# Centroid norms from matmuls, and the second pair's inputs in the set-up, in a kernel of clustered attention and two MLPs

## The chip, the core and the metric

The kernel runs on one core of a Trainium2 chip. Times are device microseconds of one execution. The kernel is compared with its changed version by the median of several executions. A profiled execution gives the trace; its times run from the start of the span, which is the first to the last instruction.

The engines are called PE (TensorE; PEld its weight loads), DVE (VectorE), ACT (ScalarE), POOL (GpSimd) and SP (SyncE, which here only issues DMAs).

## The reference

Inputs are fp32: `q`, `k`, `v` of 2 batches x 8 heads x 768 positions x 64, and 16 centroids of 64 numbers for every head. Each query and each key goes to the centroid that it is most like, and a query attends only to keys of its own cluster. Two MLPs follow, on 1536 tokens of 512 features.

```python
q_assign = np.argmax(np.einsum('bhsd,hcd->bhsc', q_n, c_n), axis=-1)   # q_n, c_n: divided by norm + 1e-6
k_assign = np.argmax(np.einsum('bhsd,hcd->bhsc', k_n, c_n), axis=-1)
mask = q_assign[:, :, :, None] == k_assign[:, :, None, :]
scores = np.where(mask, scale * np.matmul(q, k.transpose(0, 1, 3, 2)), -1e9)
attn = exp(scores - max) ; attn = attn / (sum(attn) + 1e-9)
x = (attn @ v).reshape(1536, 512)
x = silu(x @ w_in) @ w_out                    # 512 -> 2048 -> 512
out = (sigmoid(x @ w_gate) * (x @ w_val)) @ w_out2   # 512 -> 1536 -> 512
```

The choice needs the norm of each centroid only: the norm of a query changes none of its 16 products' order.

## The kernel before

**Pairs and tiles.** Two heads of one batch are a pair; there are `NPAIR` = 8. A pair's queries lie as 128 x 768 (64 features of head `j` = 0 on partitions 0 to 63, of `j` = 1 on 64 to 127). A pair has 12 tiles: 2 heads x 6 blocks of 128 queries. `scores(p, j, i)` (line 463) makes one: four matmuls into a PSUM tile `s` of two banks (high and low parts of queries and keys in `qa`, `ka`; masks and the rest in `qm`, `km`), the maximum `nm` on DVE (L476), the exponential `e` on ACT (L481). `transposes` turns `e` (PE; copied out by ACT or DVE into `ph`), `values` multiplies by `v` for three tiles at a time.

**PSUM.** Pool `ps_s` has two buffers of two banks, `ps_t` three of one bank, `ps_v` one of one bank. A tile takes a free buffer of its pool and gives it back after the last use of it in the program; the next tile waits for that. So with two buffers of `ps_s`, tile n + 2 of the scores waits for the exponential of tile n.

**Choosing clusters.** `product_of_clusters` multiplies queries and keys by the centroids `cc` (four fp32 matmuls on four column strips, L157), `scaled` applies the factor `unit` (the inverse norm of the centroid, L277), `similarities` turns the result back by three transposes (L168), and DVE picks the largest of 16 and makes one-hot rows `oh` (`first_choice` for pair 0, one head at a time; the steps of `prep(p)` at L422 for the others). `choice_rows` turns these on PE, `query_rows` and `key_rows` write them into `qm` and `km`, where they act as the mask inside the scores' matmuls.

**Set-up** (lines 186 to 621). Between `first.__enter__()` and `first.__exit__()` the instructions of PE, DVE, ACT and SP stand in their queues as written. The order on SP: `cr` (centroids, 128 KB), the first pair's queries `qq` and keys `kk`; ACT's queue loads `cc`, zero outside two blocks. Norms: `csq` = `cr` squared, summed on DVE into `n2`, the square root on ACT (L268), then six small steps on DVE to `unit` (L274). Queries and keys are split into high and low parts (`qh`, `ql`, `kh`), which SP copies into `qa`, `ka`, `qm`. `warm(n)` issues `n` matmuls of 512 columns on zeros into a PSUM tile `pw` that nothing reads (L210); `WARM` = (10, 1, 8, 5) are its four counts: at the start, behind the first product, behind `similarities`, and behind the scores of the first two tiles, which end the set-up.

**Steady part.** `one_tile` runs for the 12 tiles of each pair; only PE's order is written out there. The other engines' order is found by a scheduler that simulates, with some instructions tied behind others by `issue_after`. For pair 0, tiles 0 to 5, all that DVE gets beside the maxima stands behind tile 1's maximum. `prep(p + 1)` gets the next pair ready in steps between the tiles of pair p: POOL splits its queries and keys (L395 ff.), SP copies them, PE multiplies its clusters (`clusters`), and DVE makes the masks. The second pair's inputs are loaded by `load(1)` at the end of the set-up.

The MLPs follow on PE in a written order, with weights that are converted from the fp64 form by ACT, POOL and DVE ahead of use.

Of the kernel before, what the change touches and what calls it, by code (L numbers as in the profile page):

```python
# [27 lines left out]
WARM = (10, 1, 8, 5)  # L28
# [3 lines left out]
def clustered_attention_then_two_mlps(ctx, tc, qT, kT, v, cen, cenT, w1i, w1o, w2g, w2v, w2o, out):  # L32
    nc = tc.nc
    B, HP, _, S = qT.shape
    D = cen.shape[2]
# [73 lines left out]
    with ExitStack() as att:  # L109
# [80 lines left out]
        act_dma = nc.scalar.dma_start  # L190
        cr = cp.tile([P, HP, D], F32, tag="cr", name="cr")
        dma(cr, cen)
        cc = cp.tile([P, HP, 2, C], F32, tag="cc", name="cc")
        nc.vector.memset(cc, 0.0)
        for j, r in enumerate((L, U)):
            act_dma(cc[r, :, j], cenT[j])
# [5 lines left out]

# [3 lines left out]
        pw = ps_v.tile([P, 512], F32, tag="v", name="pw")  # L206
# [5 lines left out]
        warm(WARM[0])  # L212
# [13 lines left out]

        sq = sm.tile([P, 1], F32, tag="sq", name="sq", bufs=1)
        nc.vector.memset(sq, 1.0)
        nc.scalar.activation(sq, sq, AF.Sqrt)
# [32 lines left out]
        csq = cp.tile([P, HP, D], F32, tag="csq", name="csq")  # L262
        nc.vector.tensor_tensor(csq, cr, cr, op=ALU.mult)
        n2, r0, r1, r2, r3, r4 = (norm(f"r{n}") for n in range(6))
        unit = cp.tile([P, HP], F32, tag="unit", name="unit")
        nc.vector.tensor_reduce(n2, csq, axis=AX.X, op=ALU.add)
# [20 lines left out]
        nc.vector.tensor_tensor(km[L, 0], kk[L], kh[L], op=ALU.subtract)  # L287

        for j, (r, o) in enumerate(((L, U), (U, L))):
# [3 lines left out]
            dma(qa[o, j].bitcast(F32), ql[r].bitcast(F32))  # L293
# [12 lines left out]
        similarities(ps, sums)  # L306
        warm(WARM[2])

        chosen = []

        def first_choice(j, seen):
# [4 lines left out]
            for n in range(2):  # L316
                nc.vector.tensor_tensor(
# [4 lines left out]
                )  # L322

# [27 lines left out]
        for _ in first_choice(0, ps[:, 0:HS]):  # L351
            pass
        cast(nc.scalar, sums, ps[:, 0:HS])
# [16 lines left out]
        query_rows(0, pts[1], 0, half, half)  # L370

        on_pool = {}

        first_products = {}

        def clusters(p):
            sim = wk.tile([P, NT, 2, 2, C], F32, tag="sim", name=f"sim{p}", bufs=1)
            pm = ps_t.tile([P, 512], F32, tag="t", name=f"pm{p}")
            product_of_clusters(pm, p, *raws[p][:2])
            scaled(p, sim.rearrange("p t n j c -> p (t n j c)"), pm[:, 0:HS])  # L380
            first_products[p] = sim

        def prep(p):
# [11 lines left out]
            nc.gpsimd.tensor_scalar(qq, qq, scale, 1.0, op0=ALU.mult, op1=ALU.mult)  # L395
# [3 lines left out]
            cast(nc.gpsimd, kh, kk)  # L399
# [12 lines left out]
            sim = first_products.pop(p)  # L412
            sums = sim.rearrange("p t n j c -> p (t n j c)")
# [200 lines left out]
        if NPAIR > 1:  # L614
            load(1)
            load_values(1)
        tiles = [(p, j, i) for p in range(NPAIR) for j in range(2) for i in range(NT)]
        for t in tiles[:2]:
            scores(*t)
# [585 lines left out]
```

## Time and profile before

| | |
|---|---|
| median of 3 runs | 772.26 us (771.88 to 773.91) |
| profiled execution, span | 770.1 us; its own whole time is not listed, the median is 2.16 us above the span |
| PE busy | 760.9 us (99%) |
| DVE busy | 620.1 us (81%) |
| ACT busy | 403.4 us (52%) |
| POOL busy | 393.8 us (51%) |
| chain that ended last | PE 92%, DVE 3%, ACT 2%, DMA 1%, issue 1% |
| instructions | 11463 |

Busy time of PE counts from the start of each matmul to an end that is modelled, so that consecutive matmuls overlap: the distance of two starts is the better price of one. An idle time in brackets names the engine that ended it. The chain of waits is followed back from the last instruction to what released each step.

### The profile page before, as it was taken

What the parts mean: (1) busy time and instruction counts of PE and PEld (TensorE: products, weight loads), DVE (VectorE), ACT (ScalarE), POOL (GpSimd) and SP (SyncE); (2) the same over time, 40 slices, a digit from 0 to 9 for tenths busy, and PEclk for the clock granted to TensorE, in tenths of its full rate; (3) what the DMA queues carried; (4) which work ended last, traced back from release to release, by engine and by line L of the source; (5) the groups of instructions that cost most, each with busy time, mean ns of one, the idle gap of its engine ahead of it and who ended that gap; (6) DMA issues with size and microseconds to landing.
All of it is one profiled execution on the core that took longest, in us unless ns stands there. A gap on an engine that the chain in (4) does not pass through costs nothing.

```text
span 770.1 us, 11463 instructions
## 1 busy us (share of the span) xinstructions
PE 760.9 (99%) x4314; PEld 652.6 (85%) x4314; DVE 620.1 (81%) x787; ACT 403.4 (52%) x691; POOL 393.8 (51%) x345
## 2 busy tenths in 40 slices
PE   8999999999999999999999999999999999999998
PEld 4766777677768998998989989998998989899896
DVE  6887887788787968798978669996596997979645
ACT  6777776777886672543524516546442425344120
POOL 5235134643655773476646525644573937748320
PEclk9999999999999999999999999999999999999999
DMA  7677457447122122132222111221111221121004
GB/s 207 167 210 194 113 147 195 120 125 201 32 76 83 55 82 85 53 110 82 89 77 83 55 54 60 93 69 56 40 70 55 83 83 55 55 83 55 1 0 164
DMA packets 25488, 71.61 MB, mean 93 GB/s; under 512 B 4484, under 2 KB 4952, under 8 KB 25432
## 3 DMA queue, kind: packets, MB, share of 16 engines
q1 hardware_dynamic: 24888, 70.84, 31.1%
q8 instruction: 34, 0.56, 0.3%
q14 instruction: 22, 0.18, 0.1%
q10 hardware_dynamic: 544, 0.03, 0.0%
HBM read 48.01 MB, written 3.19 MB: 66 GB/s over the span
## 4 chain that ended last, share of the span: by engine, by line
PE 92%; DVE 3%; ACT 2%; DMA 1%; issue 1%; POOL 0%; SPq 0%; ACTq 0%
PE z L1021 13%; PE s L468 8%; PE v L518 7%; PE t L505 5%; PE y L962 4%; PE h_0w L846 4%; PE h_0x L846 4%; PE g_0w L846 3%; PE g_0x L846 3%; PE v_0w L846 3%; PE v_0x L846 3%; PE r L912 2%; PE q L912 2%; PE y_00None L962 2%; PE y_20None L962 2%; PE y_11None L962 2%
## 5 line engine op out<-in xcount | busy, mean ns | idle before, releaser
L481 ACT ACTIVATE e<-s,nm 128x768 f32<-128x768 f32 x96 | 86.5, 901 | 33.8 <-DVE nm L476 32.7
L476 DVE TENSOR_REDUCE nm<-s 128x1 f32<-128x768 f32 x96 | 91.4, 953 | 10.3 <-PE s L468 8.6
L1021 PE MATMUL z<-wu,ghb 128*128 128x512 f32 (+1 forms) x292 | 89.5, 388 | 0.0
L518 PE MATMUL v<-ph,vv 128*64 128x384 f32 x384 | 69.0, 494 | 0.2 <-DVE xf L530 0.2
L1021 PEld LDWEIGHTS z<-wu,ghb 128*128 128x128 f32 x292 | 54.2, 188 | 11.7 <-ACT ghb L64 0.6
L468 PE MATMUL s<-ka,qa 128*128 128x384 f32 x192 | 57.5, 380 | 1.7 <-ACT e L481 1.3
L505 PE MATMUL t<-ident,e 128*128 128x128 f32 x384 | 58.4, 275 | 0.1
L1021 PE MATMUL z<-wu,glb 128*128 128x512 f32 (+1 forms) x146 | 56.9, 390 | 0.0
L505 PEld LDWEIGHTS t<-ident,e 128*128 128x128 f32 x384 | 44.9, 140 | 11.3 <-issue 9.0
L518 PEld LDWEIGHTS v<-ph,vv 128*64 128x64 f32 x384 | 24.7, 136 | 32.8 <-issue 29.0
L468 PE MATMUL s<-k,q 128*128 128x384 f32 x192 | 49.7, 339 | 0.0
L942 DVE TENSOR_TENSOR acc<-z,acc 128x1024 f32<-128x1024 f32 (+2 forms) x32 | 36.6, 1152 | 13.8 <-PE z L1021 13.2
L64 ACT ACTIVATE ph<-t 128x512 f32<-128x512 f32 x68 | 40.6, 598 | 12.4 <-PE t L505 11.9
L67 DVE COPY ph<-u 128x512 f32<-128x512 f32 x48 | 32.8, 682 | 16.3 <-PE u L495 16.3
L549 POOL TENSOR_TENSOR acc<-xf,rb 128x768 f32<-128x768 f32 x7 | 12.9, 1837 | 58.5 <-DMA rb<-d_rb 40.0
L741 POOL TENSOR_TENSOR wo<-co,wo 128x512 fp32r<-128x512 f32 x16 | 23.5, 1471 | 33.6 <-ACT wo L64 33.6
L468 PEld LDWEIGHTS s<-k,q 128*128 128x128 f32 x192 | 34.5, 188 | 0.5 <-ACT k L338 0.3
L468 PEld LDWEIGHTS s<-ka,qa 128*128 128x128 f32 x192 | 28.9, 190 | 6.9 <-ACT e L481 6.0
L1021 PEld LDWEIGHTS z<-wu,glb 128*128 128x128 f32 x146 | 27.4, 188 | 6.9 <-DVE glb L902 1.4
L962 PE MATMUL y<-gha,wo 128*128 128x384 f32 x128 | 32.8, 334 | 0.0
L530 DVE TENSOR_TENSOR xf<-v,other 64x384 f32<-64x384 f32 x32 | 17.7, 553 | 14.8 <-ACT other L527 14.3
L395 POOL TENSOR_SCALAR qq<-qq 128x768 f32<-128x768 f32 x7 | 5.9, 838 | 38.2 <-PE pm L157 22.3
(629 smaller groups left out, 2160.3 us busy)
## 6 DMA issues: line engine op xcount, KB each, us to landing
ri<-in_w1i SPq DMA_DIRECT2D x16, 512.0 KB, 3.2
ro<-in_w1o SPq DMA_DIRECT2D x16, 512.0 KB, 3.2
ka<-kh SPq DMA_DIRECT2D x32, 192.0 KB, 3.4
rg<-in_w2g SPq DMA_DIRECT2D x12, 512.0 KB, 3.2
rv<-in_w2v SPq DMA_DIRECT2D x12, 512.0 KB, 3.2
ru<-in_w2o SPq DMA_DIRECT2D x12, 512.0 KB, 3.2
qq<-in_qT SPq DMA_DIRECT2D x8, 384.0 KB, 3.7
kk<-in_kT SPq DMA_DIRECT2D x8, 384.0 KB, 4.3
```

Source lines behind the costliest of these rows:

```text
L64: return nc.scalar.activation(o, i, AF.Copy)
L67: return nc.vector.tensor_copy(o, i)
L468: nc.tensor.matmul(s[:, g, 0:HS], lhsT=a[:, j, i * P : (i + 1) * P], rhs=c[:, j, g * HS : (g + 1) * HS], start=n == 0, stop=n == 1,)
L476: maxima.append(nc.vector.tensor_reduce(nm, s[:, :, 0:HS], axis=AX.XY, op=ALU.max, negate=True))
L481: x = nc.scalar.activation(e, s[:, :, 0:HS], AF.Exp, bias=nm, scale=1.0, accum_out=tots[p][:, n : n + 1])
L505: nc.tensor.transpose(t[:, kt, :], e[:, kt * P : (kt + 1) * P], ident)
L518: m = nc.tensor.matmul(o[(L, U)[kt % 2]], lhsT=vv[:, j, kt, :], rhs=ring[:, kt, g * G : (g + 1) * G], start=n < 2, stop=n >= NT - 2,)
L846: nc.tensor.matmul(o[:, b, 0:HS], lhsT=w[a][s][:, k, :], rhs=right[b, q][t][:, k, :], start=start and k == 0 and n == 0, stop=k == KQ - 1 ...
L912: nc.tensor.matmul(o[:, h, 0:HS], lhsT=w[f"a{m + 1}{r + 1}"][s][:, k, :], rhs=right[b, f"{r + 1}{h + 1}"][t][:, k, :], start=r == 0 and k ...
L942: added.append(nc.vector.tensor_tensor(z, o, z, op=ALU.add))
L962: nc.tensor.matmul(o[:, d, 0:width], lhsT=s[:, d, k, :], rhs=t[:, c], start=k == 0 and m == 0, stop=k == 1 and m == 2,)
L1021: nc.tensor.matmul(o[:, a, c], lhsT=s[:, q * P : (q + 1) * P], rhs=r[:, c], start=k == 0 and m == 0, stop=k == 1 and m == 2, skip_group_ch ...
```

## The change

- `cen` is no longer an input. `cs` loads the transposed centroids (`cenT`, 64 features x 16 centroids per pair of heads, both heads on 128 partitions); DVE copies them into the two blocks of `cc`, squares `cc`, and PE sums the squares over the partitions by multiplying with a column `one`: for each of 4 pairs of heads and each of 4 strips of 32 partitions one matmul, into the PSUM tile `n2`.
- The ten warm-ups at the start are split, five before and five behind these matmuls. `WARM` becomes (10, 1, 4, 3).
- The second pair's queries and keys are loaded right behind the first pair's, into `acc`, which is free until the attention writes there. Their product with the centroids (`ahead`) stands on PE behind the similarities of pair 0, its scaling on ACT behind the query rows, its transposes (`seen`) on PE behind the scores of tile 1, and the cast of these on DVE. `prep(1)` then leaves these steps out; `load(1)` goes.
- `pw` is a tile of `ps_s`; `ahead` is one of `ps_v`.
- The low part of the first head's keys is computed on POOL (it was DVE, L287); the first copy of `ql` is cut in two halves.
- POOL's first steps for pair 1 are tied behind the last choice mask of pair 0.

```diff
 SIGN = -0x80000000
-WARM = (10, 1, 8, 5)
+WARM = (10, 1, 4, 3)
 @with_exitstack
-def clustered_attention_then_two_mlps(ctx, tc, qT, kT, v, cen, cenT, w1i, w1o, w2g, w2v, w2o, out):
+def clustered_attention_then_two_mlps(ctx, tc, qT, kT, v, cenT, w1i, w1o, w2g, w2v, w2o, out):
     nc = tc.nc
     B, HP, _, S = qT.shape
-    D = cen.shape[2]
+    D = cenT.shape[1]
     H = 2 * HP
...
-        act_dma = nc.scalar.dma_start
-        cr = cp.tile([P, HP, D], F32, tag="cr", name="cr")
-        dma(cr, cen)
+        cs = cp.tile([P, HP, C], F32, tag="cs", name="cs")
+        dma(cs, cenT.rearrange("j d h c -> (j d) h c"))
         cc = cp.tile([P, HP, 2, C], F32, tag="cc", name="cc")
         nc.vector.memset(cc, 0.0)
-        for j, r in enumerate((L, U)):
-            act_dma(cc[r, :, j], cenT[j])
         qq = raw.tile([P, S], F32, tag="qq", name="qq0")
         dma(kk, kT[0, 0])
-
+        raws[1] = tuple(acc[:, HP - 1, n].rearrange("p b s -> p (b s)") for n in range(2))
+        for t, a in zip(raws[1], (qT, kT)):
+            dma(t, a[divmod(1, HP)])
         nc.vector.memset(wt, 0.0)
-        pw = ps_v.tile([P, 512], F32, tag="v", name="pw")
+        pw = ps_s.tile([P, 512], F32, tag="s", name="pw")
-        warm(WARM[0])
+        warm(WARM[0] // 2)
         ident = cp.tile([P, P], F32, tag="ident", name="ident")
...
+        one = sm.tile([P, 1], F32, tag="one", name="one", bufs=1)
+        nc.vector.memset(one, 1.0)
         sq = sm.tile([P, 1], F32, tag="sq", name="sq", bufs=1)
-        nc.vector.memset(sq, 1.0)
-        nc.scalar.activation(sq, sq, AF.Sqrt)
+        nc.scalar.activation(sq, one, AF.Sqrt)
...
-        csq = cp.tile([P, HP, D], F32, tag="csq", name="csq")
-        nc.vector.tensor_tensor(csq, cr, cr, op=ALU.mult)
-        n2, r0, r1, r2, r3, r4 = (norm(f"r{n}") for n in range(6))
+        for j, r in enumerate((L, U)):
+            nc.vector.tensor_copy(cc[r, :, j], cs[r])
+        csq = cp.tile([P, HP, 2, C], F32, tag="csq", name="csq")
+        nc.vector.tensor_tensor(csq, cc, cc, op=ALU.mult)
+        r0, r1, r2, r3, r4 = (norm(f"r{n}") for n in range(5))
         unit = cp.tile([P, HP], F32, tag="unit", name="unit")
-        nc.vector.tensor_reduce(n2, csq, axis=AX.X, op=ALU.add)
+        n2 = ps_t.tile([P, HP], F32, tag="t", name="n2")
+        for h in range(HP):
+            for n in range(4):
+                nc.tensor.matmul(
+                    n2[32 * n : 32 * n + 32, h : h + 1],
+                    lhsT=csq[:, h].rearrange("p j c -> p (j c)"),
+                    rhs=one,
+                    start=True,
+                    stop=True,
+                )
+        warm(WARM[0] - WARM[0] // 2)
         nc.scalar.activation(identb, ident, AF.Copy)
...
         cast(nc.scalar, kh, kk)
-        nc.vector.tensor_tensor(km[L, 0], kk[L], kh[L], op=ALU.subtract)
+        nc.gpsimd.tensor_tensor(km[L, 0], kk[L], kh[L], op=ALU.subtract)
             dma(ka[U, j].bitcast(F32), kh[r].bitcast(F32))
-            dma(qa[o, j].bitcast(F32), ql[r].bitcast(F32))
+            for c in (slice(0, HS), slice(HS, S)) if j == 0 else (slice(0, S),):
+                dma(qa[o, j, c].bitcast(F32), ql[r, c].bitcast(F32))
             if j:
...
         similarities(ps, sums)
+        ahead = ps_v.tile([P, 512], F32, tag="v", name="pm1")
+        product_of_clusters(ahead, 1, *raws[1])
         warm(WARM[2])
...
             for n in range(2):
-                nc.vector.tensor_tensor(
+                last = nc.vector.tensor_tensor(
                     oh[0][:, :, j, n, 0:C],
                 )
+            chosen.append(last)
...
             pass
+        chosen.pop()
         cast(nc.scalar, sums, ps[:, 0:HS])
...
         query_rows(0, pts[1], 0, half, half)
+        sim1 = acc[:, 0, 0, B - 1, :]
+        scaled(1, sim1, ahead[:, 0:HS])
+        first_products = {1: sim1}
-        first_products = {}
-
         def clusters(p):
-            sim = wk.tile([P, NT, 2, 2, C], F32, tag="sim", name=f"sim{p}", bufs=1)
+            sim = wk.tile([P, HS], F32, tag="sim", name=f"sim{p}", bufs=1)
             pm = ps_t.tile([P, 512], F32, tag="t", name=f"pm{p}")
             product_of_clusters(pm, p, *raws[p][:2])
-            scaled(p, sim.rearrange("p t n j c -> p (t n j c)"), pm[:, 0:HS])
+            scaled(p, sim, pm[:, 0:HS])
             first_products[p] = sim
+
+        def seen(p, sums, eng):
+
+            ps = ps_t.tile([P, 512], F32, tag="t", name=f"ps{p}")
+            similarities(ps, sums)
+            cast(eng, sums, ps[:, 0:HS])
...
-            nc.gpsimd.tensor_scalar(qq, qq, scale, 1.0, op0=ALU.mult, op1=ALU.mult)
+            with tc.issue_after(chosen[-1].ins) if p == 1 else nullcontext():
+                nc.gpsimd.tensor_scalar(qq, qq, scale, 1.0, op0=ALU.mult, op1=ALU.mult)
             cast(nc.gpsimd, qh, qq)
             yield
-            cast(nc.gpsimd, kh, kk)
+            with tc.issue_after(chosen[-1].ins) if p == 1 else nullcontext():
+                cast(nc.gpsimd, kh, kk)
             on_pool["split", p] = nc.gpsimd.tensor_tensor(kl, kk, kh, op=ALU.subtract)
...
                 clusters(p)
-            sim = first_products.pop(p)
-            sums = sim.rearrange("p t n j c -> p (t n j c)")
-            yield
-            ps = ps_t.tile([P, 512], F32, tag="t", name=f"ps{p}")
-            similarities(ps, sums)
-            cast(nc.scalar, sums, ps[:, 0:HS])
+            sums = first_products.pop(p)
+            yield
+            if p > 1:
+                seen(p, sums, nc.scalar)
             yield
...
             W = 4 * NT
-            sg = sim.rearrange("p t n j c -> p (t n j) c")
+            sg = sums.rearrange("p (w c) -> p w c", c=C)
             queued(one, nc.vector.tensor_reduce, mk[:, 0, :], sg, axis=AX.X, op=ALU.max)
...
-        if NPAIR > 1:
-            load(1)
-            load_values(1)
+        load_values(1)
         tiles = [(p, j, i) for p in range(NPAIR) for j in range(2) for i in range(NT)]
             scores(*t)
+        seen(1, sim1, nc.vector)
         warm(WARM[3])
...
         "v": v.reshape(B, H // 2, 2, S // P, P, D).transpose(0, 1, 4, 2, 3, 5),
-        "cen": np.broadcast_to(cen.transpose(1, 2, 0, 3), (2, 2, *cen.shape[1:3], H // 2, D)).reshape(P, H // 2, D),
         "cenT": cen.transpose(1, 3, 0, 2),
```

## Rows read from the trace of the kernel before

**Rows 1.** Busy time of every engine in stretches of 50 us: stretch, us busy and instructions, clock.

```profile
0.00:50.00 50.00, 45.97 (x285) 29.45 (x286) 38.49 (x95) 36.10 (x70) 21.79 (x28) 1.00 0.74 187
50.00:100.00 50.00, 50.00 (x342) 35.73 (x341) 39.46 (x57) 36.09 (x73) 16.58 (x13) 1.00 0.67 173
```

**Rows 2.** Timeline of DVE, 12 to 31.5 us: start, duration, operation, idle before it.

```profile
12.70 1.82 DVE L476 TENSOR_REDUCE nm<-s 128x1 f32<-128x768 f32 x2 [1.09 <-PE s L468]
...
15.75 0.96 DVE L476 TENSOR_REDUCE nm<-s 128x1 f32<-128x768 f32 x1 [0.29 <-PE s L468]
...
24.98 0.96 DVE L476 TENSOR_REDUCE nm<-s 128x1 f32<-128x768 f32 x1 [0.59 <-PE s L468]
...
29.02 0.94 DVE L476 TENSOR_REDUCE nm<-s 128x1 f32<-128x768 f32 x1
```

**Rows 3.** Chain that ended last, 0 to 45 us: start, duration, what ran.

```profile
13.70 1.00 ACT e L481 x2
...
14.74 0.97 PE s L468 x4
...
23.26 0.33 PE ps L168 x3
...
31.04 0.96 PE s L468 x4
```

**Rows 4.** Timeline of the first 8 us: centroid loads, first keys.

```profile
2.82 0.43 DVE L263 TENSOR_TENSOR csq<-cr 128x256 f32<-128x256 f32 x1 [0.69 <-DMA cr<-in_cen]
...
6.00 0.84 ACT L64 ACTIVATE kh<-kk 128x768 fp32r<-128x768 f32 x1 [0.30 <-DMA kk<-in_kT]
```

**Rows 5.** Timeline, TensorE: warm-ups, first product, the first tile's last wait.

```profile
1.32 4.45 PE L210 MATMUL pw<-wt 128*128 128x512 bf16 x10 [1.32 <-DVE sq L228]
...
6.28 0.48 PE L157 MATMUL pm<-qq,cc 128*32 128x384 f32 x1 [0.52 <-DMA cc<-in_cenT]
...
8.30 1.89 PE L210 MATMUL pw<-wt 128*128 128x512 bf16 x8
...
12.22 0.19 PEld L468 LDWEIGHTS s<-k,q 128*128 128x128 f32 x1 [0.26 <-ACT k L338]
```

**Rows 6.** Timeline, TensorE at 234 us: 12 small fp32 matmuls (two records each).

```profile
234.50 1.75 PE L597 MATMUL rb<-ident,rs 128*64 128x128 f32 x24
```

**Rows 7.** Timeline: weight loads of the first product.

```profile
6.25 0.14 PEld L157 LDWEIGHTS pm<-qq,cc 128*32 128x32 f32 x2 [1.39 <-DMA cc<-in_cenT]
...
6.33 0.11 PEld L157 LDWEIGHTS pm<-kk,cc 128*32 128x32 f32 x1
```

**Rows 8.** Timeline: the norms' square root, the factors, the first scaled products.

```profile
3.94 0.19 ACT L268 ACTIVATE r<-r 128x4 f32<-128x4 f32 x1
...
5.18 0.18 DVE L274 RECIPROCAL unit<-r 128x4 f32<-128x4 f32 x1
...
7.22 0.58 ACT L277 ACTIVATE sim<-pm,unit 128x384 f32<-128x384 f32 x1 [0.38 <-PE pm L157]
```

**Rows 9.** Windows of half a microsecond: last figures are DMA share and GB/s.

```profile
4.00:4.50 0.50, 0.50 (x3) 0.16 (x2) 0.30 (x2) 0.13 (x2) 0.00 (x0) 1.00 1.03 389
```

**Rows 10.** Timeline: choice rows, query rows, a copy on DVE, pair 1's product.

```profile
10.64 0.55 PE L325 MATMUL pt<-identb,oh 128*64 128x128 bf16 x7 [0.45 <-DVE oh L317]
...
12.19 0.74 ACT L328 ACTIVATE q<-pt 16x256 fp32r<-16x256 bf16 x2
...
18.82 0.68 DVE L67 COPY ph<-t 128x512 f32<-128x512 f32 x1
...
20.64 0.51 PE L157 MATMUL pm<-qq,cc 128*32 128x384 f32 x1
```

**Rows 11.** Timeline, 21 to 40 us: what follows the product, pair 1's last copy and scores.

```profile
21.42 0.44 PE L495 MATMUL u<-ident,e 128*128 128x128 f32 x2
...
29.52 0.61 SPq L408 DMA_DIRECT2D k<-kl  x1
...
36.36 0.60 PE L468 MATMUL s<-ka,qa 128*128 128x384 f32 x2
```

## The prediction

> **What bounds the kernel now.** I read the windows of 50 us first, then the chain of waits, then the timeline of the stretch where these two part. From 50 us on TensorE (PE) has no idle time, before that it has 4 us of it [rows 1]. So after the set-up and the first tiles nothing can be won or lost but by PE work, and a delay that is still there when PE becomes continuous stays to the end. The question is when that is. The chain of waits changes there: at 13.70 an exponential and at 14.74 the third tile's scores that wait for its buffer; the last such step is the scores at 31.04, behind the exponential of tile 8, and from there the chain runs on PE [rows 3]. I count the 12 tiles of pair 0 as 0 to 11. Between 12.7 and 31.04 the timeline of DVE has to be read: its maxima `nm` come behind one another with choice masks and copies between them, and it is idle for 0.29 us before tile 2's and 0.59 us before tile 7's, no more [rows 2]. So in this stretch DVE is full, PE is not, and what counts is when tile 8's maximum (29.02) runs.
>
> **The change part by part.** Sums are against the profiled execution, whose span is 770.1 us; the median of the runs is 772.26, 2.16 more for what lies around the span, which I leave as it is.
>
> *Loads.* `cr` and the small pieces of `cc` go, `cs` (128 rows of 256 bytes, 32 KB) comes. `csq` began at 2.82, when `cr` had landed, and I take that for `cs` too. The first keys, used from 6.00 [rows 4], may land up to 0.7 us earlier, with less in the queues ahead of them; that alone brings nothing, because of the next step.
>
> *Norms on PE.* DVE copies `cs` twice and squares it: `csq` cost 0.43 us for 256 columns [rows 4], so for 128 columns and two copies of 64 about 0.55, done at 3.4. On PE five warm-ups precede: ten took 4.45 us [rows 5], five end at 3.55. Then 16 fp32 matmuls of one column, on which everything on PE waits. The nearest row is line L597: 12 fp32 matmuls are 24 records in 1.75 us, 73 ns each [rows 6], on two column strips. 32 records on four strips would take 32 x 73 / 2 = 1.2 us. Below: the eight weight loads of the first product begin within 0.08 us [rows 7], which makes 0.3 us for 32. Above: 32 x 73 ns without overlap and at half the clock, 4.7 us. I take 1.2, since L597 differs only in width: until 4.75. [...]
>
> Five more warm-ups follow. [...] Three at 0.445 and two at 0.24 end at 6.55. So the product of pair 0 starts at 6.55, 0.27 later than at 6.28, whenever the keys land.
>
> *The factors.* The square root (3.94) now waits for the matmuls, 4.8; `unit` ended 1.4 us after it (5.36) and would at 6.2, before the scaled products need it (7.22 plus 0.27) [rows 8]. Hidden, with 1.3 us to spare. The casts of queries and keys behind it come up to 0.4 us later; they feed copies which are no longer the last (below).
>
> *Lower key parts on POOL* (L287), and the halved copy of `ql`. The last thing that tile 0 waited for was the key rows of the choice on ACT (L338), 0.26 us after PE was ready for them [rows 5], and not the `ql` copy. So an earlier `qa` is worth nothing. What remains of it is the choice path, behind the product: plus 0.27. Tile 0's maximum goes from 12.70 to 12.97.
>
> *Pair 1's loads and product early.* Queries and keys come in 768 KB behind the first pair's; at 389 GB/s [rows 9] that is 2 us more, landing at about 7.2. The product stands in PE's queue between the transposes of pair 0 (8.30, where warm-ups followed them [rows 5], plus 0.27: 8.6) and `warm(4)`, the choice rows and all scores. If its keys are there by then it is hidden: 0.78 us for the product and four warm-ups of 0.24 end at 10.3, before the choice rows, which were at 10.64 [rows 10] and come 0.27 later. Each microsecond beyond would be one lost for all of these. Its scaling (0.57 us) on ACT follows query rows that end at 12.93 [rows 10], now 13.2: 13.8, just before the exponential of tile 0 at 13.95. Hidden, with 0.15 to spare.
>
> *What pair 0's stretch loses.* PE: the product, 0.78 us (20.64 to 21.42) [rows 10, 11], and three transposes, 0.33 [rows 3]. ACT: a scaling and a cast. DVE gets that cast instead, right behind the first two maxima: 512 columns took it 0.68 us (18.82) [rows 10], so 384 about 0.54.
>
> *POOL's preparation of pair 1* waits now for the last choice mask, so it slips with the lag below. Its last copy is issued at 29.52, pair 1's first scores run at 36.36 [rows 11], 6.8 us later and slipping by the same lag. Hidden.
>
> *The warm-up bank.* This is the largest term, and not in the change's description. `pw` moves from pool `ps_v`, where the early product now lies, to `ps_s`, which has two buffers. Its last use, `warm(WARM[3])`, stands behind the scores of tiles 0 and 1. A buffer is given back after the last use of its tile, so while `pw` lives the scores have one buffer: tile 0 takes the one that the product of pair 0 leaves, and tile 1 must wait until tile 0 is read, which its exponential ends. In the kernel before the same wait meets tile 2, at 14.70, after an exponential of 1.00 [rows 3]. Queued behind tile 1 on PE are the transposes of `seen`, three warm-ups and all the rest; on DVE the maximum of tile 1, and behind it by order every mask of pair 0. Worked out: maximum of tile 0 12.97 to 13.93, exponential 13.95 to 14.95, scores of tile 1 from 14.99, 0.97 long [rows 3], maximum at 15.98. It was at 13.66, which is 12.70 and the 0.96 of one such maximum [rows 2]: plus 2.32. At nothing the cost is if the buffer is given back earlier; at most it is this.
>
> *The sum.* DVE starts its full stretch 2.32 late with 0.54 more to do (the cast), and has 0.88 us of idle [rows 2] to take up, the second part of which PE now fills with less work. 2.32 + 0.54 - 0.88 = 1.98 later at tile 8. PE's relief of 1.11 us lies in this same stretch, where DVE sets the pace, and is not paid out. Span 772.08, with 2.16: **774.2 us**, 0.25% more. I take no change to be what stays within 0.3%, 2.3 us, about what a measurement of this kernel can tell.
>
> **The rivals.**
>
> *A: the buffer is free for tile 1.* For it: nothing in the profile before shows `pw` holding anything. Against it: its later use. Then the maximum of tile 1 is 0.27 late, DVE adds 0.54 and takes up 0.88, and PE's relief of 1.11 can pay in part: between -0.1 and -1.2, 771.6 us.
>
> *B: slower, the clock.* Place: the product of pair 0. If PE is still at its lower level when it starts, because five of ten warm-ups have given way to almost empty matmuls, the product's 0.86 us doubles, two warm-ups take 0.2 more each and the transposes about 0.3 more: 1.5 us on the choice path, all of it before tile 0. 774.2 becomes 775.7 us. It decides from the point at which the spacing of the second five stays at 0.43 to the last. [...]
>
> *C: the lag is given back.* For it: PE has 1.11 us less to do up to tile 8, and has hardly a gap itself in the last part of this stretch; the masks on DVE could be placed behind the maxima that PE waits for. Against it: they already run wherever there is room. Then about 1 us of the lag is left: 773.2 us.
>
> **How the numbers follow.** Forecast 0.60, A 0.15, B 0.15, C 0.10. The forecast has its own range of 773.3 to 775.3 (norms 0.3 to 2 us, order on DVE); about three tenths of it lie above the bound of 774.6. Slower by over 0.3%: 0.6 x 0.3 + 0.15 x 0.95 = 0.32, and 0.01 for PE's clock falling in the wait before tile 1. Faster by over 0.3% needs A, a product no later than before and all of PE's relief, and then more: 0.06. No change 0.61. The range takes in A down to 771.0 and B up to 776.1.
>
> **What would show it.** Right: scores of tile 1 released by ACT `e` at about 15.0, a PE gap of 2 us before them, and tile 10's scores at about 33. Wrong: tile 1 directly behind tile 0 (then A); the product at 6.55 with warm-ups at 0.43 up to it (B); the product clearly before 6.28 or after 7.5, which makes the norms' price wrong; or the early product released by its keys' DMA after 9 us. The forecast falls if tile 1 does not wait.

## The result and the profile after

The changed kernel takes **781.85 us** (median of 4 runs, 779.76 to 782.56) against 772.07 for the kernel before in the same comparison: 1.0121 times as long, 95% interval 1.0103 to 1.0139. I had predicted 774.2 us and a range up to 776.1. I had given "slower by more than 0.3%" a chance of 0.33 and "no change" 0.61; a loss of this size was in none of my cases. A later set of runs of the same kernel gave 781.44 (778.23 to 781.82), 1.0115 times [1.0102, 1.0128].

The profiled run is the slowest of its four, 782.56 us with a span of 780.8, so 10.7 us more than before's 770.1. The windows of 50 us show at once that this is an affair of the first 50 us and of one place after 200 us:

```profile
0.00:50.00 50.00, 40.66 (x262) 25.90 (x267) 35.34 (x85) 30.32 (x58) 20.93 (x28) 0.97 0.59 151
50.00:100.00 50.00, 49.95 (x342) 35.79 (x343) 40.76 (x62) 36.02 (x72) 15.70 (x11) 1.00 0.66 170
...
200.00:250.00 50.00, 47.04 (x311) 34.12 (x307) 39.18 (x57) 37.87 (x75) 29.29 (x25) 0.97 0.20 63
```

TensorE (PE) lost 5.3 us of work in the first window (45.97 before [rows 1]) at a mean clock of 0.97, and from 50 us on it is full as before. So the lag has to be read tile by tile. The start of each tile's maximum `nm`, after less before, is: tile 0 +1.36, tile 1 +3.54, tile 2 +6.61, tile 8 +7.00, tile 13 +7.42, tile 94 +7.80, tile 95 +9.35. The last 1.3 us come behind tile 95, where the granted clock is 0.72 of its upper level from 238 to 244 us. I take the steps in this order.

*Set-up, +1.36.* PE's timeline of the changed kernel, start, duration, operation, and in brackets the idle time before:

```profile
1.32 2.31 PE L209 MATMUL pw<-wt 128*128 128x512 bf16 x5 [1.32 <-DVE one L227]
4.03 0.60 PE L271 MATMUL n<-one,csq 128*32 128x1 f32 x32 [0.39 <-DVE csq L265]
4.56 2.32 PE L209 MATMUL pw<-wt 128*128 128x512 bf16 x5
6.81 0.85 PE L157 MATMUL pm<-qq,cc 128*32 128x384 f32 x1
...
7.45 0.53 PE L157 MATMUL pm<-qq,cc 128*32 128x384 f32 x1
```

The norms' matmuls are short, 0.60 us. But the second five warm-ups keep the spacing of the first five, and a matmul of the product takes 0.85 us in its first pass where it took 0.48 before [rows 5]: PE is still at the lower of two paces when the product begins, and reaches the upper one in its second pass (0.53). I read the two as a lower and an upper level of PE's clock and call them so below; in the set-up that is my estimate from the times of the matmuls, since the windows list a granted clock of 1.00 from 0 to 24 us in both kernels. The scaling that waits for the product begins 0.88 us late (8.10 after 7.22 [rows 8]): 0.53 from the late start, the rest from the clock. The other 0.5 of tile 0's lag has another cause. The first masks end 1.48 us late, since they took 1.05 us for the 0.46 of before, beside POOL's first instruction for pair 1:

```profile
10.92 1.05 DVE L332 TENSOR_TENSOR oh<-wq,mw 128x96 bf16<-128x96 bf16 x2
10.98 0.89 POOL L420 TENSOR_SCALAR acc<-acc 128x768 f32<-128x768 f32 x1 [2.28 <-PE pm L157]
```

*Tile 1, another +2.18; tile 2, another +3.07.* VectorE's (DVE's) timeline:

```profile
14.07 0.96 DVE L500 TENSOR_REDUCE nm<-s 128x1 f32<-128x768 f32 x1 [0.98 <-PE s L492]
17.12 0.96 DVE L500 TENSOR_REDUCE nm<-s 128x1 f32<-128x768 f32 x1 [2.10 <-PE s L492]
18.00 0.34 DVE L173 TENSOR_REDUCE mx<-sim 128x12 f32<-128x192 f32 x1
18.26 0.55 DVE L67 COPY acc<-ps 128x384 f32<-128x384 f32 x1
18.72 0.35 DVE L176 TENSOR_TENSOR eq<-sim,mx 128x192 bf16<-128x192 f32 x1
19.10 0.76 DVE L178 TENSOR_TENSOR wq<-eq,rank 128x192 bf16<-128x192 bf16 x1
19.90 0.35 DVE L181 TENSOR_REDUCE mw<-wq 128x12 bf16<-128x192 bf16 x1
20.29 2.16 DVE L332 TENSOR_TENSOR oh<-wq,mw 128x96 bf16<-128x96 bf16 x2
22.37 1.81 DVE L500 TENSOR_REDUCE nm<-s 128x1 f32<-128x768 f32 x2
```

Tile 1's maximum waits for its scores, as forecast. What follows was not forecast. Seven instructions, the cast and the whole of the second set of choice masks, stand ahead of tile 2's maximum, and three of them are slow: `wq` 0.76 us and the two masks `oh` 2.16 together. The same `wq` and `oh` of the first set, on the same shapes in the kernel before, took 0.26 and 0.46:

```profile
9.28 0.26 DVE L178 TENSOR_TENSOR wq<-eq,rank 128x192 bf16<-128x192 bf16 x1
10.03 0.46 DVE L317 TENSOR_TENSOR oh<-wq,mw 128x96 bf16<-128x96 bf16 x2
```

GpSimd's (POOL's) timeline of that moment shows what else ran:

```profile
18.86 0.90 POOL L66 TENSOR_SCALAR qh<-acc 128x768 fp32r<-128x768 f32 x1
19.73 0.84 POOL L66 TENSOR_SCALAR kh<-acc 128x768 fp32r<-128x768 f32 x1
20.53 1.80 POOL L422 TENSOR_TENSOR ql<-acc,qh 128x768 fp32r<-128x768 f32 x1
22.29 1.81 POOL L426 TENSOR_TENSOR kl<-acc,kh 128x768 fp32r<-128x768 f32 x1
```

This is pair 1's preparation, which I had put behind the masks. Its first instruction (L420) even ran at 10.98, as shown above, just after pair 1's early product. The second mask began at 20.59 and ended at 22.44, when `ql` had ended at 22.33.

*Then the clock, +0.9 at tile 5.* (The 0.5 us that go back at tile 7 go back without a fall of the clock too, in the kernel with both repairs below.) With tile 2's maximum late, PE stands idle for 3.29 us, and the clock falls. PE's timeline, then the windows of 4 us, whose third figure from the right is the granted clock:

```profile
16.11 0.62 PE L492 MATMUL s<-ka,qa 128*128 128x384 f32 x2 [2.08 <-ACT e L505]
...
24.39 0.85 PE L492 MATMUL s<-ka,qa 128*128 128x384 f32 x2 [3.29 <-ACT e L505]
25.04 0.84 PE L492 MATMUL s<-k,q 128*128 128x384 f32 x2
```

```profile
22.00:26.00 4.00, 1.61 (x6) 1.17 (x7) 3.39 (x6) 1.88 (x4) 2.10 (x2) 0.83 0.98 222
26.00:30.00 4.00, 4.00 (x26) 3.79 (x25) 3.01 (x4) 2.38 (x6) 0.00 (x0) 0.75 1.04 242
```

A tile's scores take 1.49 us in the chain there, 0.97 before [rows 3]. The rest is small or stands elsewhere: +0.4 at tile 13, whose mask rows arrive late (PE waits 0.45 us for them), and +1.55 at tile 95, at the end of the attention.

### The profile page after: what moved, and what is told of

The parts are those of the page before. It is cut to its first block, busy times and chain, and to the rows that moved or that the text cites. A ratio compares the mean times of both kernels' runs of the same rounds, so it can differ in the third digit from the quotient of the medians.

```text
span 780.8 us, 11516 instructions
## 1 busy us (share of the span) xinstructions
PE 764.4 (98%) x4339; PEld 655.8 (84%) x4340; DVE 624.4 (80%) x788; ACT 402.9 (52%) x690; POOL 396.5 (51%) x346
## 4 chain that ended last, share of the span: by engine, by line
PE 89%; DVE 4%; ACT 2%; DMA 2%; POOL 1%; issue 1%; SPq 0%; ACTq 0%; POOLq 0%
PE z L1044 13%; PE s L492 8%; PE v L542 7%; PE t L529 5%; PE y L985 4%; PE h_0x L869 4%; PE h_0w L869 4%; PE g_0w L869 2%; PE g_0x L869 2%; PE v_0w L869 2%; PE v_0x L869 2%; PE r L935 2%; PE q L935 2%; PE y_00None L985 2%; PE y_20None L985 2%; PE y_11None L985 2%
## 5 line engine op out<-in xcount | busy, mean ns | idle before, releaser
L420 POOL TENSOR_SCALAR qq<-qq 128x768 f32<-128x768 f32 x6 | 5.0, 834 | 45.0 <-DMA qq<-in_qT 22.9
```

## Experiments

My theory after the comparison: four causes, each in its place. (1) The set-up costs 1.2 to 1.5 us, most of it by the clock and the late start of the product. (2) The warm-up bank costs some 2 us at tile 1. (3) POOL's work beside DVE's masks costs some 2 us. (4) The pause that (2) and (3) make together costs clock; no run isolates this one. The rivals are told with each run. Line numbers shift by a few between the kernels; `nm`, `oh`, `pm` are the names to follow.

### The bank alone, POOL alone, both

The first returns the warm-up buffer before the scores, by sending the last three warm-ups into the bank of the early product (which is free by then):

```diff
-        def warm(n):
+        def warm(n, into=pw):
...
-        warm(WARM[3])
+        warm(WARM[3], ahead)
```

> The changed kernel, but its last warm-ups write into the bank of the early product, so that the warm-up tile is given back before the first scores. Theory 1 (three prices: the bank's wait, POOL's work beside DVE, the late product in the set-up): tile 1's maximum is about 1.4 us late against the kernel before instead of 3.5, DVE has tile 2's maximum ahead of the one-hot masks again, but the masks stay slow beside POOL; tile 8's maximum 2.5 to 3.5 late instead of 7.0, total about 775.5 us. Theory 2 (the bank's wait is all, POOL beside DVE costs nothing that PE waits for): tile 8's maximum about 1.4 late, total 773.5. Theory 3 (the wait is harmless): total 780 or more.

The second makes the tie hold. The change asked that pair 1's preparation be issued after the last mask, but that mask is a DVE instruction, and the tie did not hold POOL, which began at 10.98. I take it that an order of issue holds only on the engine of the instruction it names. A tiny POOL copy of the last mask is an instruction of POOL's own:

```diff
+            if p == 1:
+                seen_last = sm.tile([P, NT, 1], F32, ...)
+                chosen.append(cast(nc.gpsimd, seen_last, oh[0][:, :, 1, 1, 0:1]))
             with tc.issue_after(chosen[-1].ins) if p == 1 else nullcontext():
```

> The changed kernel, but POOL's preparation of pair 1 stands behind a small POOL copy of the last one-hot mask, so that it can't run beside the masks. Theory 1: the two one-hot operations of the second head take 0.5 us each instead of 1.1, the two of the first head 0.25; tile 1's maximum still waits for the exponential of tile 0; tile 2's maximum is about 4.5 us late instead of 6.6, PE's longest gap falls from 3.3 to about 1.5 us and its clock stays up; tile 8's maximum about 4.5 late, total about 777. Theory 2 (POOL costs nothing): tile 2's maximum 6 or more late, total 780 or more.

The third has both edits.

> Both edits in the changed kernel: the bank given back early, POOL's preparation behind the last mask. Theory 1: only the set-up's delay is left, less what POOL cost the first head's masks: tile 0's maximum 0.9 us late, tile 8's 0.5 to 1.0 late, total about 772.5 to 773. Theory 4 (something else of the change holds the first tiles, such as the cast on DVE or the masks' order): tile 8's maximum 2 or more late, total over 774.

Measured, against 771.83 for the kernel before: bank 776.56 (1.0060 [1.0045, 1.0075]), POOL 777.14 (1.0071 [1.0056, 1.0086]), both 773.8 (1.0024 [1.0015, 1.0034]). Lags of the tile maxima:

| kernel | tile 0 | tile 1 | tile 2 | tile 4 | tile 8 |
|---|---|---|---|---|---|
| after | +1.36 | +3.54 | +6.61 | +6.57 | +7.00 |
| bank given back | +1.19 | +1.19 | +1.19 | +3.07 | +3.43 |
| POOL behind the masks | +1.27 | +4.03 | +4.85 | +4.56 | +4.05 |
| both | +1.55 | +1.55 | +1.56 | +1.72 | +1.22 |

With the bank given back, tile 1's wait is gone to the last hundredth. DVE's order then has tile 2's maximum ahead of `wq`, and the masks still stand still, later. DVE and POOL of that kernel:

```profile
16.95 0.96 DVE L500 TENSOR_REDUCE nm<-s 128x1 f32<-128x768 f32 x1 [0.24 <-PE s L492]
...
19.84 2.12 DVE L332 TENSOR_TENSOR oh<-wq,mw 128x96 bf16<-128x96 bf16 x2
```

```profile
20.04 1.80 POOL L422 TENSOR_TENSOR ql<-acc,qh 128x768 fp32r<-128x768 f32 x1
```

With POOL behind the masks these are fast and the bank's wait remains (tile 0 gains little from faster first masks, since here the whole product ran at the lower clock, 0.85 us a matmul in both passes), tile 1's scores now at the lower clock throughout (0.91 and 0.84 a pair of matmuls, 0.62 and 0.51 for tile 2's):

```profile
19.58 0.26 DVE L178 TENSOR_TENSOR wq<-eq,rank 128x192 bf16<-128x192 bf16 x1
...
20.26 0.43 DVE L332 TENSOR_TENSOR oh<-wq,mw 128x96 bf16<-128x96 bf16 x2
```

At tile 8 theory 1 comes near in both single repairs (2.5 to 3.5 for the bank, about 4.5 for POOL), but the clock, which it had up with POOL behind the masks, fell there. The bank alone is worth 4.05 - 1.22 = 2.83 us, POOL alone 3.43 - 1.22 = 2.21, both 7.00 - 1.22 = 5.78. The 0.74 more is what they do to each other. Falls of the clock are inside these prices: each of the two kernels has one, behind a wait of PE of 2.05 us (bank, where the four transposes of a tile then took 1.00 us for 0.60) and 2.08 us (POOL), and the one in the bank kernel is worth 0.8 us between tiles 4 and 5. So (2) and (3) are shown, and most of the loss with them.

What is left at tile 8 with both repairs is the set-up, less 0.5 us at tile 7. Both theories of that run missed: tile 0 was to be 0.9 late and the total 772.5 to 773, or tile 8 2 or more late and the total over 774. Behind tile 8 its profile, the slowest of its ten runs, loses another 1.9 us, 1.0 of it at tiles 12 and 13, where PE waits 1.04 us for mask rows; no run varied that.

### The masks beside POOL, on their own

To a kernel with both repairs (the 8 and 2 split below) this adds one subtraction of POOL, of two operands in SBUF, beside the last masks. It writes the lower key part of pair 0 once more.

```diff
+            if j == 1:
+                begin = sm.tile([P, 2 * NT, 1], F32, ...)
+                with tc.issue_after(cast(nc.gpsimd, begin, wq[:, :, 0:1]).ins):
+                    nc.gpsimd.tensor_tensor(km[U, 1], kk[U], kh[U], op=ALU.subtract)
```

> The kernel with both repairs and the 8 and 2 split, with one GpSimd subtraction of two SBUF operands (64 x 768, the lower key part of pair 0, written once more with the same values) started beside the last choice masks. Theory (VectorE's bf16 two-operand instructions stand still while GpSimd's two-operand instruction runs): the two masks take 1.5 to 2.2 us in place of 0.46 and end together with the subtraction, tile 2's maximum another 1.2 to 1.8 us later than without it; the 0.96 us maxima and the f32 copies beside GpSimd keep their times; total 773 to 775. Rival (the masks were slow in the changed kernel because of clock or semaphores, not GpSimd): masks 0.46 us, total as without it, 772.0 to 773.2.

DVE and POOL of this kernel:

```profile
16.64 0.95 DVE L507 TENSOR_REDUCE nm<-s 128x1 f32<-128x768 f32 x1
17.51 0.68 DVE L67 COPY ph<-u 128x512 f32<-128x512 f32 x1
18.11 0.96 DVE L336 TENSOR_TENSOR oh<-wq,mw 128x96 bf16<-128x96 bf16 x2
```

```profile
16.96 1.82 POOL L332 TENSOR_TENSOR k<-kk,kh 64x768 fp32r<-64x768 f32 x1
```

The maximum and the copy from PSUM beside the subtraction keep their times. The first mask stands from 18.11 to 18.90 (0.80 us, 0.25 alone); the subtraction ends at 18.79. As DVE's order brought the masks only near the end of the subtraction, the price is 0.55 us and not the 1.2 to 1.8 I had written; the lag rises by 0.71 from tile 3 to tile 4 (0.16 without the subtraction). The total, 773.13 (1.0017 [1.0008, 1.0026]), is too near to its neighbour to say more. The mechanism is confirmed for the one mask that met the subtraction, the size I had put on this run was wrong.

### The changed kernel once more

> The changed kernel once more, unchanged. Theory (the 1.75 us lost at tile 95 and the 0.95 after it, at the seam of the attention, come from a fetch of instructions that happened to collide with one landing): the profile shows the same 7 us at tiles 8 to 94, and at the seam either nothing more or another sum; most times between 779.5 and 782.6. Rival (the seam's loss belongs to the change): tile 95's maximum again 1.5 us later than tile 94's lag, and all times within 0.3 of 781.9.

It took 781.44, with lags +1.25, +4.02, +8.11, +8.51 (tiles 0, 1, 2, 8) and +9.38 at both 94 and 95. So the step at tile 95 is not in every run of the change, while the loss in the first tiles is itself not fixed, as my theory had it: here the masks met both of POOL's subtractions, and the clock fell in the wait ahead of tile 1 (0.93 and 0.84 us a pair of matmuls, 0.62 and 0.51 for tile 2's).

```profile
15.99 0.93 PE L492 MATMUL s<-ka,qa 128*128 128x384 f32 x2 [2.07 <-ACT e L505]
16.71 0.84 PE L492 MATMUL s<-k,q 128*128 128x384 f32 x2
```

```profile
20.76 3.18 DVE L332 TENSOR_TENSOR oh<-wq,mw 128x96 bf16<-128x96 bf16 x2
```

```profile
20.20 1.84 POOL L422 TENSOR_TENSOR ql<-acc,qh 128x768 fp32r<-128x768 f32 x1
22.00 1.82 POOL L426 TENSOR_TENSOR kl<-acc,kh 128x768 fp32r<-128x768 f32 x1
```

The first mask ended 0.1 us after `ql`, the second began and ended 0.1 us after `kl`. Why the first run lost 1.55 us at tile 95 stays open: a row of `rb` landed over 2 us, with a fetch of instructions beside it, but no run varied that. The runs' mean clocks say something of (4): of the nine runs of the changed kernel, eight had 0.995 or 0.996 and took 779.76 to 782.56, and one had 1.0 and took 778.23.

### The norms alone, and the place of the warm-ups

The kernel before with the norms by matmul and nothing else of the change:

> The kernel before with the norms by matmuls alone: the one centroid load, the copies on DVE, five warm-ups before and five behind the 16 matmuls; nothing of pair 1 is early, the warm-up tile stays where it was, its counts too. Theory 1: the first product starts about 0.5 us late and at PE's lower clock, tile 0's maximum is 0.9 late, and that lag stays to the end: total about 773.0. Theory 5 (the set-up has room for it): tile 0's maximum at most 0.3 late, total 772.2.

774.82 (1.0036 [1.0023, 1.0048]), more than either theory; tile 0 to tile 28 are +1.44 late, and the chain has the product wholly at the lower clock, 1.51 us against the 0.86 of before:

```profile
6.88 1.51 PE pm L157 x8
```

So (1) is shown, at 1.44 us: 0.60 is the later start of the product (6.28 before), 0.65 its lower clock. The rest of the total arises later, 1.2 us at tile 29 and 0.7 at tile 95. No run varied either. In all six profiles with the 5 and 5 split (the changed kernel twice, the bank, POOL, both, this one) the product's first pass ran at 0.85 us a matmul. Next, both repairs with the warm-ups split 8 and 2 about the norms:

```diff
-        warm(WARM[0] // 2)
+        warm(8)
...
-        warm(WARM[0] - WARM[0] // 2)
+        warm(WARM[0] - 8)
```

> Both repairs (warm-up buffer given back early, GpSimd behind the last mask) with the norms by matmul, the ten warm-ups split 8 and 2 about the norms' matmuls instead of 5 and 5. Theory (PE's pause of 0.5 us and the 0.6 us of one-column matmuls in the middle of the warm-ups keep the clock at its lower level until after the product): eight warm-ups end at 4.9, the norms at 5.5, two more at 6.4 or sooner, the product of pair 0 runs at the upper clock (0.86 us, not 1.5), tile 0's maximum 0.1 to 0.6 us late instead of 1.55, total 772.3 to 773.0. Rival (any one-column matmuls ahead of the product cost the clock, wherever they stand): the product still takes 1.5 us, tile 0's maximum 1.3 us late or more, total 773.6 to 774.2.

772.5, 1.0006 [0.9997, 1.0015]: no difference to before that these runs can tell, and 1.3 us less than with 5 and 5. Its product begins 0.46 us sooner, and the clock rises in the middle of it (0.85 us a matmul in the first pass, 0.63 in the second):

```profile
1.32 3.60 PE L209 MATMUL pw<-wt 128*128 128x512 bf16 x8 [1.32 <-DVE one L227]
...
6.35 0.85 PE L157 MATMUL pm<-qq,cc 128*32 128x384 f32 x1
```

The kernel with the added subtraction has the very same set-up, and there it rose during the eight warm-ups:

```profile
1.32 3.23 PE L209 MATMUL pw<-wt 128*128 128x512 bf16 x8 [1.32 <-DVE one L227]
4.48 0.43 PE L271 MATMUL n<-one,csq 128*32 128x1 f32 x32
...
5.38 0.51 PE L157 MATMUL pm<-qq,cc 128*32 128x384 f32 x1
```

Tile 0 is +0.51 in the one and -0.53 in the other. The moment of the rise is not set by the program alone; of one set-up a single profile shows one throw (norms at 0.43 from 4.48 in the one, a product still at 0.85 from 6.35 in the other).

I then tried to make the thin stretch shorter: 4 norm matmuls of 128 columns instead of 16 of 32, once with the 8 and 2 split, once behind all ten warm-ups.

```diff
-            for n in range(4):
-                nc.tensor.matmul(n2[32 * n : 32 * n + 32, h : h + 1], lhsT=csq[:, h] ..., rhs=one, ...)
+            nc.tensor.matmul(n2[:, h : h + 1], lhsT=csq[:, h] ..., rhs=one, ...)
```

> Both repairs and the 8 and 2 split, with the norms in 4 fp32 matmuls of 128 columns instead of 16 of 32 (the squares are written four times over by one VectorE instruction). Theory (the length of the thin stretch on PE is what delays the clock's rise: 0.54 us of it kept the first half of pair 0's product at the lower clock): the norms take 0.1 to 0.2 us, the product starts at 6.2 and runs at the upper clock for most of its length, under 1.0 us, tile 0's maximum 0 to 0.25 us late, total 771.6 to 772.3. Rival (a thin stretch of any length there, or too few warm-ups after it, keeps the clock down): the product takes 1.2 us or more and tile 0 stays 0.4 us late or more, total 772.4 to 773.

> As the kernel with 4 wide norm matmuls, but these stand behind all ten warm-ups, directly ahead of pair 0's product. Theory (ten unbroken warm-ups bring the clock up before the product, as in the kernel before): norms at 5.8 to 5.95, product at 6.2 at the upper clock (0.86 us), its scaling waits for the factors until about 7.35, tile 0's maximum 0.1 to 0.2 us late, total 771.6 to 772.2. Rival (thin matmuls right ahead of the product cost the clock most): the product at 1.3 us or more, tile 0 0.5 us late or more, total 772.4 to 773.

772.6 (1.0011 [1.0002, 1.002]) and 774.36 (1.003 [1.0019, 1.0042]). Both expectations failed at their first number; the totals are the rival's for the first and above both for the second. Tile 0 is +1.60 and +3.10. The second kernel's PE:

```profile
1.32 4.45 PE L209 MATMUL pw<-wt 128*128 128x512 bf16 x10 [1.32 <-DVE one L227]
5.56 1.71 PE L271 MATMUL n<-one,csq 128*128 128x1 f32 x8
7.20 0.85 PE L157 MATMUL pm<-qq,cc 128*32 128x384 f32 x1
```

Eight records of 128 columns take 1.71 us, 32 of 32 columns took 0.60. So the stretch became longer, not shorter, and in both profiles the whole product ran at the lower clock, 0.85 us a matmul in both passes. In that profile ten unbroken warm-ups did not suffice when thin matmuls followed.

### The early work without the matmul norms

Both repairs, with the norms, warm-ups and centroid loads of before:

> The change without its norms by matmul: the centroids' norms on VectorE, the ten warm-ups and the loads of the centroids are those of the kernel before; the early load, product and similarities of pair 1 stay, the warm-up buffer is given back before the first scores, and GpSimd's preparation of pair 1 really stands behind the last choice mask. Theory (the matmul norms cost 1.2 to 1.5 us at tile 0, all of it the clock and the set-up; bank and GpSimd cost the rest): tile 0's maximum within 0.2 us of before, the product of pair 0 at 6.3 at the upper clock, tile 8's maximum 0 to -0.5, total 771.5 to 772.5. Rival (the early load or product itself costs what is still late in the kernel with both repairs): tile 0's maximum 0.5 us late or more, total 773.3 to 774.

774.5 (1.0032 [1.002, 1.0043]): the rival's number, with a cause that neither had.

```profile
7.44 0.48 PE L157 MATMUL pm<-qq,cc 128*32 128x384 f32 x1 [2.18 <-DMA cc<-in_cenT]
...
7.80 0.63 PE L157 MATMUL pm<-kk,cc 128*32 128x384 f32 x1
```

The product begins only at 7.44, at the upper clock, and the clock falls in its second pass (0.63 us a matmul after 0.48; pair 1's product behind it took 1.44 us, 0.85 in the next kernel), behind 2.18 us in which PE did nothing; tile 0 is +1.71. Of its seven runs one had a mean clock of 1.0 and took 771.98, the others (0.994 to 0.999) 773.49 to 775.63, so the fall has a large part in the 774.5. The product waits for the two small centroid transfers that ScalarE issues: in the kernel before the product waits for them as well, until 6.28 [rows 5], and now pair 1's 768 KB are loaded beside them. So one load of the centroids ahead of all else, the part of the change that I had priced at nothing, is what the early loads need. Putting the two together, without the norms by matmul:

```diff
-        for j, r in enumerate((L, U)):
-            act_dma(cc[r, :, j], cenT[j])
+        cs = cp.tile([P, HP, C], F32, tag="cs", name="cs")
+        dma(cs, cenT.rearrange("j d h c -> (j d) h c"))
...
+        for j, r in enumerate((L, U)):
+            nc.vector.tensor_copy(cc[r, :, j], cs[r])
```

> As the kernel with both repairs and the norms of before on VectorE, but the block-diagonal centroids are no longer two small transfers issued by ScalarE: the transposed centroids come in one 32 KB transfer ahead of the queries, and VectorE copies them into place after the norms' sums. Theory (in the kernel before it those small transfers landed at 7.3 behind the early loads, and that alone held the product of pair 0): the product starts at 6.2 to 6.4 after ten unbroken warm-ups and takes 0.86 us at the upper clock, tile 0's maximum within 0.2 us of before, tile 8's -0.4 to 0, total 771.3 to 772.0. Rival (the early loads hold the first queries and keys too, or the pause ahead of the product costs the clock): the product at 6.8 or later or at 1.3 us, tile 0 0.5 us late or more, total 772.4 to 774.5.

```profile
1.32 4.39 PE L211 MATMUL pw<-wt 128*128 128x512 bf16 x10 [1.32 <-DVE sq L229]
5.64 0.83 PE L157 MATMUL pm<-qq,cc 128*32 128x384 f32 x2
```

The product now begins at 5.64, 0.64 us before that of the kernel before; tile 0 is -0.29, tile 8 -0.64, tile 95 -0.45. The profiled run took 771.44, the median is 772.04 (771.44 to 775.71), 1.0008 times before [0.9999, 1.0018]. Product and tile 8 come earlier than my theory had them (6.2 to 6.4, -0.4 to 0), the total is just above its range. It takes back what the change lost and wins nothing that can be measured: 0.6 us of lag is less than its runs differ by.

## Why the prediction was wrong

**The step that failed** is the paragraph on POOL: "*POOL's preparation of pair 1* waits now for the last choice mask, so it slips with the lag below. [...] Hidden." Both halves are wrong. It did not wait: the tie names an instruction of DVE, and POOL began pair 1's scaling at 10.98, as soon as the early load and the early product let it. And it was not hidden: I had asked who waits for POOL's results, and not whom POOL's running slows. This is worth 2.2 us with the bank free, and 3.0 on top of the bank (7.00 - 4.05).

It is not the only step. The kernel with POOL behind the masks is the one that I had described, and it took 777.14 us, still above my range. At its tile 8 it has 4.05 where I had 1.98: 1.00 more at tile 0 (the late product and its clock), 0.71 more at tile 1 (the clock fell in the wait for the bank), and 0.36 more behind tile 1, where my sum gave 0.34 back and this kernel nothing. These terms are told below.

The slow ones here (`wq` 0.76 for 0.26, a mask 1.85 for 0.25) have two inputs in SBUF. So has a slow f32 one: in the same profile a DVE subtraction of two SBUF operands (`xt`, 128 x 768) took 1.50 us at 264.20 beside POOL's work, and 0.94 at 273.60 with POOL idle. `eq`, with two f32 inputs, kept its 0.35 us at 18.72, but POOL's scaling began only at 18.86, 0.14 us into it. Beside POOL's fills a `wq` kept 0.26 us (15.21 in the kernel before).

The other steps in their order:

- *Loads.* `cs` was there by 2.41 (I said 2.82). Right that this brings nothing at tile 0; wrong to price the one load at nothing, since the early loads need it, as the run without it shows.
- *Norms.* Done by 4.63 and not 4.75. The matmuls took 0.60 us, half my 1.2. No run shows the 2 us at the top of the range that I gave them: the 32 records took 0.43 to 0.61 us. L597 was a poor neighbour: it differs not only in width, since its matmuls have 128 moving columns and the norms one. But the copies and the square ended at 3.97 and not 3.4: two copies of 64 columns took 1.24 us, the second 0.80 in the chain, beside POOL's fills.
- *The clock at the product.* I took it to be up, at 6.55, as if it rose at the same moment as before, and gave no reason. The sum's three warm-ups at 0.445 us and two at 0.24 came in no profile with this split: the second five took 2.32 us, as the first five did (2.31). Rival B had it down, with a chance of 0.15, and B's sign was there to see: warm-ups at 0.43 to the last. Tile 0 came 1.36 late and not 0.27, 0.5 of that by the slow first masks. B had 1.5 us more than the forecast at tile 0; the six profiles with this split have 0.9 to 1.3 more, the late copies included.
- *Factors, the early product and its scaling:* hidden, right. `unit` ended at 6.17. But the loads were not there at about 7.2: the product began at 9.27 and waited for its keys until 10.04, one of my signs of being wrong (after 9 us). It stayed hidden only because the rest was late too: the warm-ups behind it end at 11.86, and the choice rows, at 10.64 before, start at 12.11.

```profile
10.04 0.15 PEld L157 LDWEIGHTS pm<-acc,cc 128*32 128x32 f32 x6 [0.64 <-DMA acc<-in_kT]
```

- *The warm-up bank.* Right in place, cause and size. Tile 1's scores were released by the exponential of tile 0, after a PE gap of 2.08 us; 2.18 us on top of tile 0's lag, where I had 2.05 (2.32 - 0.27; with the start of before read as 13.58 and not 13.66, 2.13). In the two profiles in which the clock fell in that wait (the changed kernel once more, POOL behind the masks) it is 2.77 and 2.76. Rival A fell.
- *The cast on DVE*, 0.54 us: it took 0.55 and cost nothing where the bank was free, since tile 2's maximum waits another 0.24 us for its scores.
- *DVE full, PE's relief not paid out.* Only partly: with both repairs the lag falls by 0.5 us at tile 7, into the idle time that I had seen [rows 2], and it does not fall there in the kernel with the norms alone, whose PE has no relief. Rival C's mechanism is real and small.
- *The sum.* I moved DVE's stretch as a block. But with the bank held DVE's order is another one: the cast and the masks come ahead of tile 2's maximum, worth 0.8 us with fast masks (tile 1 to tile 2 in the table), which are back by tile 8. I had nothing for that, and 0.01 of chance for the fall of PE's clock in the wait before tile 1. It came there in the second profile, and in the first one in the longer wait after tile 2.

So, of the 7.00 us at tile 8: set-up and what is given back 1.22, bank 2.83, POOL 2.21, the two together 0.74. I forecast 1.98, nearly all of it the bank. The second profile has 8.51 there, so these are the sizes of one profile each; and the 3.6 us that the first profile lost behind tile 8 are explained only in part.

## What to carry to other kernels

When a change moves work on an engine earlier, ask what will then run beside it, even if nobody waits for its result; list the neighbours that its running may slow as one lists those that share its queue (here two masks of 0.46 us took 2.16 beside POOL's subtraction). An order that named DVE's last mask (to 22.44) did not hold POOL here, which began at 10.98; one that named a POOL copy did (20.95): look at the first start of the engine that is meant to be held. And a wait of 2 us in a static order is not a shift by 2 us, since it changes what stands ahead of the next maximum and may let PE's clock down, as 2.07 and 2.08 us did in two profiles here.

## What the runs showed of the hardware

- A DVE mask of 96 bf16 elements with both inputs in SBUF, 0.25 us alone, took up to 1.86 us beside a two-operand subtraction of POOL, and ended about 0.1 us after that, in four profiles of three kernels. Beside it, f32 maxima (0.96) and copies from PSUM (0.68) kept their times.
- fp32 matmuls of one moving column: 32 records of 32 weight columns, on four column strips, 0.60 us behind warm-ups that came every 0.43 us, and 0.43 where the clock had risen; 8 records of 128 weight columns 1.71 us. Many narrow ones were far cheaper than a few wide.
- PE's rise to its upper pace came during the warm-ups in one profile (norms at 0.43 us from 4.48) and at least 2.5 us later in another of the same set-up (a product still at 0.85 us a matmul from 6.35); with ten unbroken warm-ups the product began at the upper pace (0.48 to 0.51 us a matmul) in the three profiles in which no thin matmuls followed them, and at the lower (0.85) in the one in which they did.
- Waits of PE of about the same length did and did not bring the clock down: 2.08 us left it up in the first profile of the changed kernel (the next pair of matmuls took 0.62 us), 2.07 and 2.08 us were followed by a fall in two others (0.93 and 0.91).
